# Batch 0's q and k loaded in two parts of tokens, its v loads cast on the way, and batch 1's x transposed pair by pair, in a fused attention and MLP kernel

## The chip, the cores and the metric

The kernel runs on one core of a Trainium2 chip. The metric is the device time of one execution in microseconds. Five instruction streams run beside each other and are tied by semaphores: TensorE (PE, with its weight loads shown as PEld), VectorE (DVE), ScalarE (ACT), GpSimd (POOL) and SyncE (SP). Transfers between HBM and the core's memory are issued from the streams of SP, ACT and POOL and are moved by 16 DMA engines. Each stream executes its instructions in the order in which the program lists them.

## The reference

Causal attention with 16 extra keys and values ("beacons") ahead of the sequence, then a two-layer MLP with a squared relu:

```python
B, H, S, Nb, D = (8, 8, 576, 16, 64)          # q, k, v: B x H x S x D, float32
k_all = concatenate([beacon_k, k], axis=2)
v_all = concatenate([beacon_v, v], axis=2)
scores = matmul(q, k_all.T) / sqrt(D)          # token i sees the 16 beacons and the tokens 0 to i
a = softmax(scores)
attn = matmul(a, v_all)                        # heads side by side: x is 4608 x 512
out = (relu(x @ w_in) ** 2) @ w_out            # w_in 512 x 2048, w_out 2048 x 512
```

## The kernel before, in words

The program is not written in the order in which it runs. Each piece of work is an `Op` with the engines that may do it, an assumed duration, a priority, the ops that it needs and the buffers that it takes (`Order.add`, L149). `Order.run` (L155) plays the ops through with these assumed durations and emits the instructions in the order that this gives, so a duration in the code (`act`, L384; `cost` values in the `add` calls) sets only the order of the streams. What really happens is timed by the semaphores between the instructions.

The work per batch `b` is four pairs of heads (`pr`, two heads of 64 make 128 columns).

- **q and k of batches 0 to 2** are loaded "strided" (`add_strided`, L580): partition `p` of 96 holds the six tokens 6p to 6p+5 of a head, so that a run in HBM is 1536 bytes. Batch 0's first pair comes by one load from SP and one from ACT as float32 (L592); the other pairs by one k and one q load each on POOL's queue, which cast to bf16 (L599, six loads for batch 0). PE transposes each pair (`tp`: L638 with 64 columns each for batch 0's pairs 1 to 3, L635 with 128 columns where DVE or ACT has first regrouped the two heads, the "spin" of L623), DVE copies the k half to `kT` (L650) and DVE or ACT the q half to `qT` (L655); all copies show line L437 (ACT) or L439 (DVE, POOL).
- **v** comes in five tiles of 128 keys (`add_load`, L468). Batch 0's tiles 0 to 2 are issued by SP (L483 the beacon, L484), tiles 3 and 4 and all of batch 1's by POOL (`SOFT_V`, L457). All land as float32 in one of eight staging buffers (`stg`) and are then cast into `vb` by POOL, tiles 0 and 1 of batch 0 by POOL or DVE (L508). `vb` has 65 columns per head, the last one ones, so that the product also gives the softmax sum.
- **Scores** (L764), exp on ACT (L781), causal mask on DVE (L799, L803), the product with v on PE (`av`, L819), division on DVE (L834, L835) into `xn`. Batch 0 alone is split in two phases (`SPLIT`, L686): phase 0 covers the tokens 0 to 239 and needs v tiles 0 and 1, phase 1 the rest and all five tiles.
- **x**: `xn` has to be transposed into `xT`. Batch 0 does it on PE (`add_xt_pe`, L873: transposes L883, copies L895), batches 1 to 7 by DMA transposes issued from SP, one for each of five token tiles and all four pairs (`add_xt`, L859).
- **MLP** in nine chunks of 512 tokens (`add_chunk`, L922). "s1" multiplies x by w_in (L947) in 16 blocks of 128 hidden columns, relu on ACT (L964) or DVE (L966), square on DVE (L973); "s2" multiplies by w_out (L987). Chunk 0's s1 is cut at token 240 like batch 0's phases. w_in and w_out each come in four loads on POOL's queue (L908, L917); a quarter of w_in is four blocks of s1.

Two things fix the order of POOL's stream around the start. The loads of batch 0's q and k have priorities near -200 and go first; `TURNS` (L306) chains what follows: `win0`, the v tiles 3 and 4, `win1` to `win3`, then batch 1's beacon, k, q and v, then w_out, then batch 2. And `win0` carries an explicit wait (`sync`, L911) until the last q load of batch 0 has landed, v tile 0 one until pair 1's q has landed (L1072). Where the plan finds PE idle between its microseconds 10 and 22 it puts in products of the identity that nobody reads ("fill", L526, lines L533 to L537).

## Time and profile before

| | |
|---|---|
| median of three runs | 338.75 us (338.75 to 340.36) |
| the profiled execution's own time | 338.65 us |
| its span in the trace | 336.9 us |
| busy in the span: PE, ACT, DVE, POOL | 327.1, 193.6, 160.5, 86.8 us |
| HBM read, written | 37.22 MB, 9.44 MB |
| granted TensorE clock | 1.00 throughout |

A row of a timeline or of the chain of waits is: start in us, length in us, engine, line of the code, operation, what it writes and reads, how often (xN), and in brackets how long the engine had stood idle before it and what ended that. The chain of waits follows the last instruction back, at each step to what released it. A row of the table by stretches gives for each engine the busy us and the number of instructions. "SPq" and "POOLq" are the streams that issue transfers. The time outside the span is 338.65 - 336.9 = 1.75 us.

### The profile page before, as it was taken

What the parts mean: (1) busy time and instruction counts of PE and PEld (TensorE: products, weight loads), DVE (VectorE), ACT (ScalarE), POOL (GpSimd) and SP (SyncE); (2) the same over time, 40 slices, a digit from 0 to 9 for tenths busy, and PEclk for the clock granted to TensorE, in tenths of its full rate; (3) what the DMA queues carried; (4) which work ended last, traced back from release to release, by engine and by line L of the source; (5) the groups of instructions that cost most, each with busy time, mean ns of one, the idle gap of its engine ahead of it and who ended that gap; (6) DMA issues with size and microseconds to landing.
All of it is one profiled execution on the core that took longest, in us unless ns stands there. A gap on an engine that the chain in (4) does not pass through costs nothing.

```text
span 336.9 us, 7692 instructions
## 1 busy us (share of the span) xinstructions
PE 327.1 (97%) x3172; PEld 184.2 (55%) x3172; DVE 160.5 (48%) x323; ACT 193.6 (57%) x300; POOL 86.8 (26%) x135
## 2 busy tenths in 40 slices
PE   3999999999999999999999999999999999999995
PEld 2778766545545555554468845545554544444444
DVE  6669977267604761475245632673246503301400
ACT  3887974597457647465656745755656226515611
POOL 7765911425122605140512351220000000000000
PEclk9999999999999999999999999999999999999999
DMA  9999999699959999799989996991310041011003
GB/s 167 196 207 210 206 203 207 147 247 179 221 104 223 241 199 176 185 208 228 206 121 257 242 210 138 209 196 32 104 62 2 14 120 63 0 62 64 0 17 110
DMA packets 138211, 50.38 MB, mean 150 GB/s; under 512 B 124176, under 2 KB 133264, under 8 KB 138176
## 3 DMA queue, kind: packets, MB, share of 16 engines
q1 hardware_dynamic: 128304, 40.42, 57.7%
q0 software_dynamic: 9520, 9.11, 16.3%
q8 instruction: 25, 0.41, 0.6%
q10 hardware_dynamic: 352, 0.36, 0.4%
q14 instruction: 10, 0.08, 0.1%
HBM read 37.22 MB, written 9.44 MB: 138 GB/s over the span
## 4 chain that ended last, share of the span: by engine, by line
PE 93%; DMA 2%; POOL 1%; DVE 1%; issue 1%; ACT 0%; POOLq 0%
PE ps L947 37%; PE ps L987 36%; PE ps L819 9%; PE ps L764 8%; DMA qk_area<-in_q_dram 2%; PE ps L635 1%; PE ps L1030 1%; POOL qk_area L599 1%; PE ps L883 1%; DVE g L966 0%; PE ps L537 0%; POOL vb L439 0%; PE ps L533 0%; POOL w_in L908 0%; DVE g L973 0%
## 5 line engine op out<-in xcount | busy, mean ns | idle before, releaser
L947 PE MATMUL ps<-xT,w_in 128*128 128x512 bf16 (+3 forms) x704 | 133.7, 340 | 0.2
L987 PE MATMUL ps<-w_out,g 128*128 128x512 bf16 x560 | 128.4, 379 | 0.0
L781 ACT ACTIVATE pt<-ps 128x1024 bf16<-128x1024 f32 (+3 forms) x128 | 102.9, 874 | 18.3 <-PE ps L764 18.1
L947 PEld LDWEIGHTS <-w_in 128*128 128x128 bf16 x704 | 65.9, 98 | 55.2 <-issue 3.9
L964 ACT ACTIVATE g<-ps 128x512 bf16<-128x512 f32 (+2 forms) x116 | 65.5, 568 | 39.1 <-PE ps L947 38.6
L987 PEld LDWEIGHTS <-g 128*128 128x128 bf16 x560 | 52.1, 98 | 61.1 <-issue 3.6
L973 DVE TENSOR_TENSOR g<-g 128x1024 bf16<-128x1024 bf16 (+2 forms) x80 | 52.1, 654 | 69.6 <-ACT g L964 69.4
L437 ACT COPY osb<-ps 128x512 f32<-128x512 f32 (+2 forms) x37 | 21.3, 576 | 68.8 <-PE ps L987 54.6
L439 POOL CAST qk_area<-stg 128x512 bf16<-128x512 f32 (+2 forms) x50 | 34.2, 688 | 67.5 <-DMA stg<-in_q_dram 41.0
L439 POOL CAST vb<-stg 128x512 bf16<-128x512 f32 (+1 forms) x39 | 26.1, 675 | 63.3 <-DMA stg<-in_v_dram 63.2
L799 DVE TENSOR_TENSOR pt<-pt,tri 128x1024 bf16<-128x1024 bf16 (+1 forms) x36 | 23.5, 654 | 34.2 <-ACT pt L781 34.2
L819 PEld LDWEIGHTS <-pt 128*128 128x128 bf16 (+1 forms) x960 | 34.2, 98 | 6.3 <-ACT pt L781 0.4
L966 DVE TENSOR_SCALAR g<-ps 128x512 bf16<-128x512 f32 (+2 forms) x44 | 26.8, 611 | 19.7 <-PE ps L947 19.4
L819 PE MATMUL ps<-vb,pt 128*128 128x65 bf16 (+1 forms) x960 | 35.6, 195 | 0.4 <-POOL vb L439 0.3
L764 PE MATMUL ps<-qT,kT 64*128 64x80 bf16 (+6 forms) x680 | 32.9, 235 | 0.0
L764 PEld LDWEIGHTS <-kT 64*128 64x128 bf16 x680 | 19.0, 96 | 16.8 <-issue 13.8
L835 DVE TENSOR_TENSOR xn<-ps,rcp 128x640 bf16<-128x640 f32 (+2 forms) x36 | 27.0, 750 | 1.8 <-DVE rcp L834 0.5
L834 DVE RECIPROCAL rcp<-ps 128x10 f32<-128x10 f32 (+2 forms) x36 | 7.5, 209 | 28.9 <-PE ps L819 28.9
L437 ACT COPY qT<-ps 128x576 bf16<-128x576 bf16 x12 | 7.6, 644 | 8.4 <-PE ps L635 7.4
L803 DVE TENSOR_TENSOR pt<-pt,tri 80x160 bf16<-80x160 bf16 x32 | 11.1, 347 | 0.0
L439 DVE COPY kT<-ps 128x576 bf16<-128x576 bf16 x12 | 8.9, 751 | 1.8 <-PE ps L638 1.2
L635 PE MATMUL ps<-ident,sparek 96*128 96x96 bf16 x18 | 1.5, 229 | 5.8 <-DVE sparek L439 5.8
(52 smaller groups left out, 80.4 us busy)
## 6 DMA issues: line engine op xcount, KB each, us to landing
out_dram<-osb SPq DMA_DIRECT2D x17, 512.0 KB, 3.6
stg<-in_v_dram SPq DMA_DIRECT2D x20, 256.0 KB, 5.1
stg<-in_q_dram SPq DMA_DIRECT2D x20, 256.0 KB, 5.5
stg<-in_k_dram SPq DMA_DIRECT2D x15, 256.0 KB, 4.3
w_in<-in_moe_w_in_dram POOLq DMA_DIRECT2D x4, 512.0 KB, 8.8
w_out<-in_moe_w_out_dram POOLq DMA_DIRECT2D x4, 512.0 KB, 11.6
stg<-in_v_dram SPq DMA_DIRECT2D x7, 224.0 KB, 4.5
qk_area<-in_k_dram POOLq DMA_DIRECT2D x4, 288.0 KB, 11.5
```

The source lines that it names most:

```text
L437: nc.scalar.copy(dst, src)
L439: eng[e].tensor_copy(dst, src)
L764: nc.tensor.matmul(st[:, hj, lo + col:lo + col + t1 - t0], kT[x.b % 2][hp, x.pr, 128 * c:128 * c + 128], qT[x.b % 2][hp, x.pr, t0:t1], sta ...
L781: nc.scalar.activation(pt[x.take_pt.held[0]][:, :, off:off + width], pair(box["qk"], k)[:, :, lo:lo + width], AF.Exp, bias=0.0, scale=scale)
L799: nc.vector.tensor_tensor(out=d, in0=d, in1=tri[:, m0:m0 + m, :][:, None].to_broadcast([128, 2, m, 128]), op=ALU.min)
L819: nc.tensor.matmul(a[:, hj, (t - tl[0]) * (D + 1):(t - tl[0] + 1) * (D + 1)], P[0:rr, hj, o:o + 128], vb[b % 2][0:rr, c, h, :], start=(c = ...
L835: nc.vector.tensor_tensor(out=xn[b % 2].rearrange("p t (h d) -> p h t d", d=D)[:, 2 * pr:2 * pr + 2, tl[0]:tl[0] + nt], in0=a[:, :, :, 0:D ...
L947: nc.tensor.matmul(h[:, lo - spans[0][0]:hi - spans[0][0]], w_in_sb[:, mc, ft * 128:(ft + 1) * 128], xT[:, mc, lo % RING:lo % RING + hi - lo],
L964: nc.scalar.activation(dst, h, AF.Relu, bias=0.0, scale=1.0)
L966: nc.vector.tensor_scalar(out=dst, in0=h, scalar1=0.0, scalar2=None, op0=ALU.max)
L973: nc.vector.tensor_tensor(out=d, in0=d, in1=d, op=ALU.mult)
L987: nc.tensor.matmul(o, G[:, fc, ts * 128:(ts + 1) * 128], w_out_sb[:, fc, :], start=(fc == 0), stop=(fc == NFT - 1))
```

## The change

It edits the start of the kernel and some bookkeeping:

- Batch 0 leaves `add_strided` for a new `add_first`. Its q and k come in two parts of tokens: part a, the tokens 0 to 239 on 40 partitions, part b, the tokens 240 to 575 on 56 partitions. Part a of the first pair comes from SP and ACT as before, part a of pairs 1 to 3 by one k and one q load on POOL; part b by four loads on POOL (pairs 0 and 1, pairs 2 and 3). There is one set of transposes and two copies for each pair and part. Scores of phase 0 need part a alone, those of phase 1 also part b.
- All v loads of batches 0 and 1 are issued by POOL and cast on the way into `vb` (whose rows become 66 columns per head); the staging buffers and the casting instructions fall away for them.
- `TURNS` now orders POOL's queue from the start, with v tiles 0 and 1 between the two parts and `win0` between the two halves of part b. The explicit waits of `win0` and of v tile 0 are gone.
- Unread products start at the plan's microsecond 0.6 instead of 10, before 2.6 as 512-column products of a zeroed area of `xT` ("hot", one more DVE memset).
- Batch 1's x is transposed pair by pair, three DMA transposes for each pair (12 in place of 5), each after that pair's division alone. `xn` is laid out by pairs for it.
- Batch 2's regrouping copies go from DVE to POOL. Some assumed durations of the plan are new.

```diff
-    FILL = (10.0, 22.0)
+    FILL = (0.6, 22.0)
...
-TURNS = ("win0 ld0v3 ld0v4 win1 win2 win3 bkl1 sld1k0 sld1q0 sld1k2 sld1q2 ld1v0 ld1v1 ld1v2 ld1v3 ld1v4 "
-         "wout0 wout1 wout2 wout3 bkl2 sld2k0 sld2q0 sld2k2 sld2q2")
+TURNS = ("sld0k1a sld0q1a ld0v0 ld0v1 sld0k0b sld0q0b win0 sld0k2b sld0q2b ld0v2 ld0v3 ld0v4 win1 win2 win3 bkl1 sld1k0 sld1q0 sld1k2 sld1q2 ld1v0 ld1v1 ld1v2 ld1v3 ld1v4 wout0 wout1 wout2 wout3 bkl2 sld2k0 sld2q0 sld2k2 sld2q2")
...
-    vb = [sb(f"vb{i}", [128, NT, H, D + 1], BF16) for i in range(2)]
+    vb = [sb(f"vb{i}", [128, NT, H, D + 2], BF16) for i in range(2)]
...
-        return 0.066 + n / 1200.0
+        return 0.105 + n / 1190.0
...
+    hot = xT[:, 0, 0:512]
+    nc.vector.memset(hot, 0.0)
...
+    XPAIR = 1
-    SOFT_V = [(0, 3), (0, 4)] + [(1, c) for c in range(NT)]
+    SOFT_V = [(b, c) for b in range(2) for c in range(NT)]
+    FIRST_GROUPS = [(1, 4)]
+    SECOND_GROUPS = [(0, 2), (2, 4)]
...
+            def emit_soft(e):
+                to = vb[b % 2][:, c, :, 0:D]
+                insts = []
+                if lo:
+                    insts.append(queue.dma_start(out=to[0:Nb], in_=beacon[b].transpose([1, 0, 2])))
+                insts.append(queue.dma_start(out=to[lo:rows], in_=t[b, :, t0:t0 + rows - lo, :].transpose([1, 0, 2])))
+                return insts
...
+        if now < 2.6:
+            def emit(e):
+                nc.tensor.matmul(ps[:, 7, :], hot[:, 0:128], hot, start=True, stop=True)
...
+    PARTS = [(0, 40), (240, 56)]
+    P0 = PARTS[0][1]
...
+        for n, x in enumerate("kq"):
+            def emit(e, x=x):
+                queue = nc.sync if e == "SP" else nc.scalar
+                return [queue.dma_start(out=first[x], in_=src_of[x][0, 0:2, 0:P0 * NS].rearrange(
+                    "h (p s) d -> p h s d", s=NS))]
...
+        for u, groups in ((0, FIRST_GROUPS), (1, SECOND_GROUPS)):
+            tok, parts = PARTS[u]
+            for lo, hi in groups:
+                for x in "kq":
+                    def emit(e, x=x, lo=lo, hi=hi, u=u, tok=tok, parts=parts):
+                        return [nc.gpsimd.dma_start(
+                            out=at[x][u][0:parts, 2 * lo:2 * hi],
+                            in_=src_of[x][0, 2 * lo:2 * hi, tok:tok + NS * parts].rearrange("h (p s) d -> p h s d", s=NS))]
...
+                tp = add(f"tp0.{pr}{'ab'[u]}", "PE", 0.3 if turned else 0.35, emit_tp,
+                         prio=100.0 * pr - 190 + 1000.0 * u, deps=need + [ident_op], take=("ps", "tp", [1]),
+                         mode="full" if turned else "columns")
...
+                spin[x].append(add(f"spin{b}{x}{pr}", "POOL" if b == 2 else "DVE", {"POOL": 0.85, "DVE": 0.45}, emit_spin,
...
+            if b == 0:
+                late_deps[p] = [trans[0, "k"][HP + pr], trans[0, "q"][HP + pr]]
...
+    def add_xt_pairs(b):
+        at = (b * S) % RING
+        for pr in range(HP):
+            for n, (lo, hi) in enumerate(((0, 1), (1, 4), (4, 5))):
...
+                    nc.sync.dma_start(out=dst, in_=area[0:rows, 128 * (NT * pr + lo):128 * (NT * pr + hi)], transpose=True)
...
+                        deps=[norm_ops[HP * b + pr, 0]] + ring_deps(b * S + t0, b * S + t0 + cols), dma=0.16 * cols / 128,
...
-            w_ops["in", i] = add(f"win{i}", "POOL", 0.95, emit, prio=-100 + i, sync=[strided[0][HP - 1, 'q']] if i == 0 else (),
+            w_ops["in", i] = add(f"win{i}", "POOL", 0.95, emit, prio=-100 + i, 
...
-                if c == 0:
-                    sync = [strided[0][HP - 3, "q"]]
+                pass
...
-            add_xt(b)
+            (add_xt_pairs if b == XPAIR else add_xt)(b)
...
-    named["ld1v0"].behind.append(named["cast0v4"])
```

More of the change, by code (lines that the diff above doesn't have):

```diff
@@ L537, in emit @@
                     nc.tensor.matmul(ps[:, spot, 0:128], ident, ident, start=True, stop=True)
-        op = Op("fill", "PE", 0.11, emit, mode=mode)
+        op = Op("fill", "PE", 0.22 if now < 6.0 else 0.11, emit, mode=mode)
         op.left, op.held = 0, None
@@ L589, in add_strided @@
[L589 to L595 removed]
+        step = 2
+        for pr in range(0, HP, step):
@@ L713 @@
     norm_ops = {}
+    late_deps = {}
     def add_pair(b, pr):
```

150 lines of the change are left out of this document (106 added, 44 removed).

## The prediction

> **What bounds the kernel now.** First the table by stretches and one row of PE's timeline:
>
> ```profile
> 0.00:19.59 19.59, 13.28 (x188) 10.14 (x188) 12.75 (x45) 12.36 (x18) 13.60 (x27) 1.00 0.99 185
> 19.59:46.25 26.66, 26.49 (x406) 20.87 (x403) 23.76 (x61) 22.50 (x43) 17.75 (x25) 1.00 1.22 207
> 46.25:66.00 19.75, 19.75 (x248) 11.79 (x246) 11.44 (x27) 9.41 (x15) 5.44 (x10) 1.00 1.00 180
> ```
>
> ```profile
> 19.59 0.99 PE L947 MATMUL ps<-xT,w_in 128*128 128x240 bf16 x8
> ```
>
> I cut the stretches at 19.59 us, where the first product of the MLP runs, and at 46.25 us, where s2 of chunk 0 begins. From 19.59 us on PE is busy without a gap (26.49 of 26.66 us, then 19.75 of 19.75). Before it PE runs 188 instructions in 19.59 us, against 406 in the next 26.66. So time can be won almost only ahead of 19.59 us, and what is won there stays won as long as PE never lacks work later. The chain of waits over the first 20 us says what sets 19.59 (its first line gives shares of these 20 us):
>
> ```profile
> by line: DMA qk_area<-in_q_dram 28.3%; POOL qk_area L599 14.8%; issue 11.2%; PE ps L764 6.5%; PE ps L819 5.8%; PE ps L883 5.5%; PE ps L537 5.3%; POOL vb L439 4.4%; PE ps L533 3.9%; POOL w_in L908 3.9%; DVE xn L835 2.2%; PE ps L947 2.1%; POO
> ...
> 4.99 5.65 DMA qk_area<-in_q_dram
> 10.64 0.29 issue
> 10.93 0.77 POOL w_in L908
> ...
> 12.60 0.88 POOL vb L439
> 13.48 0.04 issue
> 13.52 0.50 PE ps L819 x6
> ```
>
> POOL's stream stood at `win0` until the last q had landed, so its cast of a v tile came at 12.60, and PE's first product with v at 13.52. From there to the MLP are 6.07 us (19.59 - 13.52), of which about 1.85 us are unread products (L537 and L533, 5.3% and 3.9% of 20 us).
>
> **Part 1: q and k in two parts.** Timelines of DVE, of ACT (one row) and, from 2 to 4 us, what the DMA engines moved:
>
> ```profile
> 1.57 0.27 DVE L410 MEMSET bks<- 128x256 uint32 x1
> 1.92 0.59 DVE L411 MEMSET tri<- 128x640 bf16 x1
> 2.48 1.65 DVE L416 MEMSET pt<- 128x96 uint32 x12
> 5.19 0.56 DVE L439 CAST sparek<-g 96x768 bf16<-96x768 f32 x1 [1.05 <-DMA g<-in_k_dram]
> ```
>
> ```profile
> 8.88 0.79 ACT L781 ACTIVATE pt<-ps 128x736 bf16<-128x736 f32 x1
> ```
>
> ```profile
> DMA packets 383, 0.52 MB, mean 259 GB/s; under 512 B 48, under 2 KB 383, under 8 KB 383
> ```
>
> The first pair's two loads are 2 x 2 x 576 x 64 x 4 bytes = 0.59 MB, 2.3 us at 259 GB/s; part a is 240/576 of it, 0.25 MB or 0.95 us. So it lands 1.3 us earlier, 3.9 instead of 5.19. But DVE's memsets end at 2.48 + 1.65 = 4.13, and the change adds one of the size of the 0.27 us row: DVE is free at 4.4. The regrouping copies (0.56) then end at 5.0, 0.8 us sooner than now. Two copies of 240 columns in place of 576 save about as much again, so the first exp comes near 7 instead of 8.88. Part a of pairs 1 to 3 is 6 heads x 240 x 64 x 2 bytes each of k and q, 0.37 MB in bf16, which the 0.82 MB in 4 us of a row below moves in 1.8 us: from 4 to 6, seen near 7, all three together, where the last q now lands at 10.64. All this lies ahead of the v tiles below and is hidden by them: it sets nothing unless v comes more than 2 us earlier than I reckon.
>
> [...] No row of before shows a 40-partition load.
>
> The part b transposes are added PE work: 24 more instructions for each pair.
>
> ```profile
> 32.22 0.51 PE ps L635 x12
> ```
>
> That is a pair of batch 1: twelve transposes of 96 columns, all 128 wide. Batch 0's pairs 1 to 3 have 24 of half the width; split in 40 and 56 columns a pair costs 0.51 again if columns count, 1.02 if instructions do. Of four pairs two fall behind the start of the MLP; I charge **0.6 us** (0 to 1.0).
>
> **Part 2: POOL's queue.** It now reads: k and q of part a; identity (0.30); mask matrix `tri` (priority -150, so ahead of v, 1.48); v tile 0 with its beacon; v 1; part b of pairs 0 and 1; `win0`; part b of pairs 2 and 3; v 2 to 4; `win1` to `win3`. POOL's timeline has the prices:
>
> ```profile
> 2.85 0.30 POOL masks.py:199 TENSOR_SCALAR_AFFINE_SELECT ident<-ident 128x128 bf16<-128x128 bf16 x1
> ...
> 5.88 1.48 POOL L424 TENSOR_SCALAR_AFFINE_SELECT tri<-tri 128x128 bf16<-128x128 bf16 x5
> 10.93 0.77 POOL L908 DMA_DIRECT2D w_in<-in_moe_w_in_dram  x1 [3.56 <-DMA qk_area<-in_q_dram]
> 11.70 0.91 POOL L484 DMA_DIRECT2D stg<-in_v_dram  x1
> ```
>
> The first two issues end ahead of the identity, as now. `tri` therefore ends at 2.85 + 0.30 + 1.48 = 4.63, the beacon at 5.2, v 0 is issued 5.2 to 6.1 and v 1 to 7.0 (0.91 each). How long until bytes flow? `win0` was issued at 10.93:
>
> ```profile
> q1 hardware_dynamic: 1318, 0.33, 83.7%
> q0 software_dynamic: 5, 0.00, 1.1%
> ```
>
> ```profile
> q1 hardware_dynamic: 709, 0.18, 41.1%
> q0 software_dynamic: 96, 0.10, 39.9%
> ```
>
> These are the queues at 10 to 12 and at 12 to 14 us (packets, MB, share of the 16 engines); q1 is SP's, q0 POOL's. POOL's queue moves five packets in the first and a 40% share in the second, so it begins near 13.0, 2.1 us after the issue. v 0 thus flows from 7.3. **A casting v load** is not in the trace. Bounds: below, bytes of the bf16 side at the rate of the other casting loads; above, SP's v loads, 0.33 MB in 2 us, which is 1.55 us for 256 KB. POOL's queue from 32 to 36 us, mostly uncast v loads, and from 20 to 24 us, casting loads of weights and k:
>
> ```profile
> q0 software_dynamic: 294, 0.84, 104.0%
> ```
>
> ```profile
> q0 software_dynamic: 830, 0.82, 124.0%
> ```
>
> 0.84 MB in 4 us is 1.25 us for 256 KB; 0.82 MB is 0.63 us for 128 KB. I take 1.25: the source still comes in runs of 256 bytes. v 1 then ends near 9.9 and is seen 0.8 us later (the first pair's k was moved by 4.4 and landed at 5.19), at **10.8**. No cast follows, so PE's product with v starts at 10.8 instead of 13.52: 2.7 us earlier (9.5 to 12.0 by the bounds and one us on the start).
>
> [...]
>
> **Part 3: from v to the MLP.** The 6.07 us shrink by what of the 1.85 us of unread products isn't needed, and grow where DVE now makes part b's copies in the same stretch. I take 5.3 (4.2 with all the fill gone, 7.0 with four copies of some 0.4 us on the path): the MLP starts at 16.1 instead of 19.59, a **lead of 3.5 us** (0.6 to 4.7; `win0`, issued 8.2, is served behind v 0, v 1 and part b until 14.1 and lands near 14.9).
>
> **Part 4: does PE stay fed?** Until 22 us only a quarter of w_in is there. On POOL's timeline:
>
> ```profile
> 24.94 0.85 POOL L484 DMA_DIRECT2D stg<-in_v_dram  x1 [1.91 <-DMA w_in<-in_moe_w_in_dram]
> 27.44 2.73 POOL L484 DMA_DIRECT2D stg<-in_v_dram  x3 [1.65 <-DMA w_in<-in_moe_w_in_dram]
> ...
> 31.96 0.80 POOL L917 DMA_DIRECT2D w_out<-in_moe_w_out_dram  x1 [0.36 <-DMA qk_area<-in_k_dram]
> 33.59 1.55 POOL L917 DMA_DIRECT2D w_out<-in_moe_w_out_dram  x2 [0.82 <-DMA qk_area<-in_q_dram]
> ```
>
> ```profile
> DMA to landing us min/median/max: 9.8/11.6/13.8
> ```
>
> POOL stands at 24.94 and 27.44 for w_in, at 31.96 and 33.59 for batch 1's k and q, each the eighth load back. The queue is at its rate (207 GB/s from 19.59 on), so what counts is bytes ahead. They are the same in both orders; the slack at 10 to 14 us (0.33 and 0.28 MB in 2 us each, against 0.41) goes, and a like one opens between part a, served by 6, and v 0 at 7.3. So `win2` and `win3` (24.9, 27.4), batch 1's k and q (32.0, 33.5) and the first of w_out stay within 0.5 us of now. In the lead, from 16.1 to 22, PE has two pairs' part b (1.0), eight or nine pieces of phase 1's scores (the chain's four at L764 take 6.5% of 20 us, so 2.6 to 2.9), four blocks of s1 (16 products, 1.8 by the row of 19.59), and products with v once tiles 2 to 4 are in near 19.7: about 6 us of work for 6. I charge **0.2 us** (0 to 2). Later, s2 starts at 46.25 - 2.7 = 43.5 and needs w_out's first quarter, which lands at 41.8 now (issued 31.96, and the second fence gives the four w_out loads' time to landing; the first has the least, 9.8). Batch 1's x:
>
> ```profile
> xT<-xn SPq DMA_TRANSPOSE x35, 2.5
> ```
>
> ```profile
> 58.99 6.50 SPq L866 DMA_TRANSPOSE xT<-xn  x5
> ```
>
> ```profile
> 67.05 1.03 PE L947 MATMUL ps<-xT,w_in 128*128 128x512 bf16 x4
> ```
>
> The fourth of five, the last that chunk 1 needs, is issued from 62.9 (58.99 + 3 x 1.3) and lands 2.5 us later at 65.4, 1.6 us ahead of chunk 1's first product at 67.05. Moved forward by 2.7 us, PE would wait for it by 1.1 us if batch 1 did not move too; of twelve smaller ones only three stand behind the last division, some 3.9 us of SP's stream if each costs the 1.3 of now, instead of 5.2 for four. That edit is therefore worth 0 to 1.1 us, and I count it as cover. SP has nothing else queued there but batch 3's loads.
>
> Batch 2's regrouping on POOL (eight copies) is covered: POOL is busy 5.44 of 19.75 us there and loses five casts. The new durations of the plan change orders only; 0.5 us either way. The unread products run while PE has nothing else; one of 512 columns, under 0.5 us, could stand ahead of a real one, covered by the v tiles. If they bring a faster clock to the first transposes, that too lies ahead of v; the granted clock is 1.00 in every row of the table, so nothing shown here prices it. The 66-column rows are never read at their end: 0.
>
> **The sum.** 338.65 - 3.5 + 0.6 + 0.2 = **335.95**, say 335.9; the profiled execution is 0.10 us below the median of 338.75. With the bounds of the terms its own range is 334.6 to 337.4.
>
> **Rivals.**
>
> 1. *Casting halves the v loads.* At 0.63 us each v 1 is seen 1.2 us earlier and `win0` too; the lead grows to its limit of 4.7, less 0.6 of transposes: 338.65 - 4.1 = 334.5. For it: all other casting loads run at their bf16 bytes. Against: those come in runs of 1536 bytes.
> 2. *The lead is eaten before `win1`.* Phase 1 has twelve exps of some 0.85 us (8.88: 0.79 for the smaller ones), 10 us of ACT from near 12.6; if PE's stream stands behind them and v tiles 2 to 4 for 2 us more than charged, 338.65 - 2.7 + 2 = 338.0. For it: ACT's load; against: ACT is busy 12.36 of the first 19.59 us, so it has room.
> 3. *One queue, slower v loads: slower than before.* If a casting load costs twice 1.25 us (each run written in two steps), ten of them stand ahead of w_out, whose first quarter lands at 41.8 + 12.5 = 54.3, and PE, out of work near 46.25, waits until then: +8, up to 346. It decides where ten loads eat the slack of 46.25 - 41.8 = 4.4 us, from 1.7 us a load. Against: the dearest row is 1.55.
> 4. *The order doesn't come out as written*, because the plan's streams misjudge the chip and PE sits behind a late instruction: the gain of rival 2, counted there.
>
> **How the numbers follow.** Forecast 0.5, rival 1 0.2, rivals 2 and 4 0.17, rival 3 0.13. A measurement can tell 0.5% (1.7 us) from no change: faster means under 337.0. Faster: nearly all of the forecast's half and rival 1, 0.7; same: the upper end of the forecast and rival 2, 0.17; slower: rival 3, 0.13. The range takes in rivals 1 and 2 with their bounds and the near edge of 3: 333.2 to 338.7.
>
> **What would show it.** Right: first product with v (L819) near 10.8 with no cast ahead, first L947 near 16, s2 (L987) near 43.5, and from there the same lead to the end; POOL's queue near 200 GB/s from 7 us on. Part 1 is wrong if the first exp comes after 8; part 2 if a v load takes much over or under 1.25 us or `tri` is not ahead of v 0; part 3 if L947 starts after 17.5; part 4 if PE shows gaps between 16 and 27 us or ahead of chunk 1. The forecast falls if the lead at the first L947 is not the lead at the end, or if w_out lands after s2 could start.

## The result, and the profile after

The changed kernel is slower: 343.39 us (341.11 to 344.67) beside 339.22 us (338.75 to 340.36) for the kernel before, a ratio of 1.0121 (95% interval 1.0091 to 1.0152). The prediction was 335.9 us in a range of 333.2 to 338.7. The profiled execution took 342.73 us with a span of 341.0 us, 4.1 us more than before's 336.9, and the reading below follows these 4.1 us.

The changed kernel by stretches, cut where the first product of the MLP runs, where s2 of chunk 0 begins and where chunk 1 begins:

```profile
0.00:18.87 18.87, 16.38 (x263) 12.07 (x264) 11.39 (x44) 8.83 (x17) 14.89 (x28) 0.82 1.16 131
18.87:48.30 29.43, 29.43 (x494) 23.48 (x492) 25.38 (x69) 25.38 (x45) 13.51 (x19) 1.00 1.45 197
48.30:69.07 20.77, 20.55 (x249) 12.01 (x250) 9.79 (x19) 10.07 (x16) 11.25 (x17) 1.00 0.89 147
```

The MLP starts at 18.87 instead of 19.59: a lead of 0.7 us, not 3.5. From there to s2 it takes 29.43 us instead of 26.66, and s2 starts 2.05 us late (48.30 against 46.25). PE is "busy" in all 29.43 us, with 494 instructions where before had 406. This is the first thing to see: the busy share does not show the loss, because other work fills it. The 88 more are 48 transposes of part b, 20 unread products and 20 products of scores; the last are scores of phase 1, which before ran ahead of the MLP. PE's work on scores in this stretch, of the changed kernel (104 by its weight loads) and of before (84):

```profile
18.87:48.30 29.43, 6.38 (x104) 2.93 (x104) 1.00 1.45 197
19.59:46.25 26.66, 4.78 (x88) 2.30 (x84) 1.00 1.22 207
```

The chain of waits over the same 29.43 us stays on PE alone, so here nothing but PE's own stream of work sets when s2 starts:

```profile
by line: PE ps L1070 50.8%; PE ps L861 18.6%; PE ps L916 13.0%; PE ps L734 7.0%; PE ps L565 5.4%; PE ps L665 3.0%; PE ps L1006 2.0%; PE ps L597 0.3%
```

Chunk 1 starts 2.02 us late (69.07 against 67.05), and chunk 2 4.06 us late. These are the rows of chunk 2 on PE's timeline, of before and of the changed kernel:

```profile
105.04 2.33 PE L947 MATMUL ps<-xT,w_in 128*128 128x512 bf16 x10
```

```profile
109.10 3.18 PE L1070 MATMUL ps<-xT,w_in 128*128 128x512 bf16 x13 [1.54 <-DMA xT<-xn]
```

Behind chunk 2 the two kernels run alike: 341.0 - 109.10 = 231.9 us against 336.9 - 105.04 = 231.9. So there are two losses, about 2.0 us up to s2 and another 2.0 us between chunk 1 and chunk 2.

The chain of waits of the changed kernel over its first 20 us:

```profile
by line: DMA qk_area<-in_q_dram 28.1%; PE ps L565 22.2%; PE ps L665 13.7%; PE ps L861 12.1%; issue 5.7%; PE ps L916 5.1%; PE ps L1006 4.0%; PE ps L1070 3.6%; POOL qk_area L631 2.5%; POOLq L1251 0.1%
...
7.91 0.36 PE ps L665 x12
8.28 0.34 PE ps L861 x4
...
10.44 0.97 PE ps L565 x8
11.41 0.72 PE ps L861 x6
12.13 1.18 PE ps L565 x10
13.32 0.66 PE ps L916 x12
13.98 1.74 PE ps L565 x20
```

L565 is the unread product, L665 a transpose of q and k, L861 the scores, L916 the product with v. POOL's wait for q and the cast of v are gone from the chain, as predicted. In their place stands PE's own stream: 22.2% of 20 us, 4.4 us, are unread products, which PE executes in the order of the plan whether or not v has landed. Ahead of all this stands the first pair's regrouping, which ends at 5.79:

```profile
4.96 0.83 ACT L438 CAST sparek<-g 40x768 bf16<-40x768 f32 x1 [2.01 <-DMA g<-in_k_dram]
```

**The first loss** is seen best on ACT. First before, then the changed kernel (L781 and L878 are the exps; four in phase 0 of batch 0, with 736 columns, then twelve in phase 1, with 832 or 928; a row's shape is that of its first instruction):

```profile
12.45 3.23 ACT L781 ACTIVATE pt<-ps 128x736 bf16<-128x736 f32 x4
16.76 0.36 ACT L437 COPY xT<-ps 128x240 bf16<-128x240 bf16 x1 [1.09 <-PE ps L883]
17.56 3.30 ACT L781 ACTIVATE pt<-ps 128x832 bf16<-128x832 f32 x4 [0.44 <-PE ps L764]
...
25.93 1.94 ACT L781 ACTIVATE pt<-ps 128x928 bf16<-128x928 f32 x2
```

```profile
11.87 1.46 ACT L878 ACTIVATE pt<-ps 128x736 bf16<-128x736 f32 x2 [0.60 <-PE ps L861]
15.86 0.36 ACT L438 COPY xT<-ps 128x240 bf16<-128x240 bf16 x1 [2.53 <-PE ps L1006]
...
18.01 3.43 ACT L878 ACTIVATE pt<-ps 128x832 bf16<-128x832 f32 x4
...
21.94 2.61 ACT L878 ACTIVATE pt<-ps 128x928 bf16<-128x928 f32 x3
24.94 1.70 ACT L878 ACTIVATE pt<-ps 128x928 bf16<-128x928 f32 x2 [0.39 <-PE ps L861]
27.27 1.70 ACT L878 ACTIVATE pt<-ps 128x832 bf16<-128x832 f32 x2 [0.63 <-PE ps L861]
29.57 0.86 ACT L878 ACTIVATE pt<-ps 128x832 bf16<-128x832 f32 x1 [0.59 <-DVE rcp L931]
```

Before, the row at 12.45 holds three exps of phase 1: their scores ran while PE waited for v, and the first of the three starts at 13.3. In the changed kernel the first exp of phase 1 comes at 18.01. ACT does no exp between 13.3 and 18.0, stands still for 2.53 us of it, and then needs until 29.57 + 0.86 = 30.4 for the same twelve; before they ended at 25.93 + 1.94 = 27.9. That is 2.6 us later, at the place where PE needs them for its products with v.

Two things hold these scores back. One is POOL's queue, where part b stands behind v. The last load that pairs 0 and 1 need (q, issued at 7.78) lands 5.2 us after its issue, at 13.0, where before the last q of all was in at 10.64:

```profile
L631 POOL DMA_DIRECT2D qk_area<-in_q_dram x1: 659/659/659, 7.8 to 7.8; - x1
DMA to landing us min/median/max: 5.2/5.2/5.2
```

The other is PE's own order: the transposes of this part b come only at 15.93, some 3 us after it has landed, behind the product with v and the unread products of the chain above. From the transposes to the exp are 2.1 us (18.01 - 15.93). Had they followed the landing at once, the exp would have come near 15.1, an estimate from these rows; of the 4.7 us by which it is later than before, 1.8 would then be the queue's and 2.9 those of PE's order. (In the kernel a2 below, which has no unread products, these transposes come at 14.2 and the exp at 17.3, and the granted clock rises only at 25.6.) Pairs 2 and 3 are alike: landed at 17.9 (issued at 9.85, 8.1 us), transposed from 20.46.

PE's rows there, of the changed kernel:

```profile
15.93 0.56 PE L665 MATMUL ps<-ident,qk_area 56*64 56x56 bf16 x24
...
16.82 0.56 PE L665 MATMUL ps<-ident,qk_area 56*64 56x56 bf16 x24
...
20.46 0.94 PE L665 MATMUL ps<-ident,qk_area 56*64 56x56 bf16 x48
...
22.86 0.50 PE L565 MATMUL ps<-ident 128*128 128x128 bf16 x6
...
25.33 0.73 PE L565 MATMUL ps<-ident 128*128 128x128 bf16 x10
```

Part b's transposes, 2.06 us in all, now lie on PE's path to s2, where before all of q and k was transposed by 11.8 us, ahead of v. And between 22.9 and 25.9 PE fills in unread products. The second quarter of w_in was no help: POOL, which stands until it has landed, went on at 23.69 instead of 22.5 or earlier, and at 26.24 and 28.83 (before 24.94 and 27.44) for the third and fourth:

```profile
23.69 0.54 POOL L490 DMA_DIRECT2D vb<-in_beacon_v_dram  x1 [0.84 <-DMA w_in<-in_moe_w_in_dram]
```

**The second loss** shows on SP. Its stream in the changed kernel (L988: batch 1's x by pairs, L963: batch 2's by tiles), then before (L866: both by tiles):

```profile
46.52 8.59 SPq L988 DMA_TRANSPOSE xT<-xn  x6
...
57.72 3.99 SPq L988 DMA_TRANSPOSE xT<-xn  x3
...
65.06 4.60 SPq L988 DMA_TRANSPOSE xT<-xn  x3
...
94.71 5.67 SPq L505 DMA_DIRECT2D stg<-in_q_dram  x4
...
101.32 7.71 SPq L963 DMA_TRANSPOSE xT<-xn  x5
```

```profile
92.34 7.84 SPq L866 DMA_TRANSPOSE xT<-xn  x5
```

Twelve transposes by pairs take 8.59 + 3.99 + 4.60 = 17.2 us of SP's stream; five by tiles took 6.50 us. One transpose took much the same time whether by pair (one or three blocks of 128 columns; least, median and most in ns below) or by token tile (1250 to 1283 ns), but for two of 2.07 us:

```profile
L988 SPq DMA_TRANSPOSE xT<-xn x12: 1093/1236/2072, 46.5 to 68.4; - x12
```

Batch 2's x starts at 101.32 instead of 92.34, 9.0 us later, and chunk 2 waits 1.54 us for it. SP is one reason for these 9.0 us, and not the larger. Batch 2's last division, before and in the changed kernel:

```profile
90.03 0.82 DVE L835 TENSOR_TENSOR xn<-ps,rcp 128x640 bf16<-128x640 f32 x1
95.96 0.82 DVE L932 TENSOR_TENSOR xn<-ps,rcp 128x640 bf16<-128x640 f32 x1
```

It comes 5.9 us later, so batch 2's attention is itself late. Behind it SP takes 4.5 us until it turns to this x (101.32 - 96.78), before 1.5: the other 3.0 us are SP's written order, which now has later loads (94.71 to 101.2) ahead of it. Why batch 2's attention falls back more than s2 did was not tested.

### The profile page after: what moved, and what is told of

It is laid out like the page before. It is cut to its first block, busy times and chain, and to the rows that moved or that the text cites. A ratio compares the mean times of both kernels' runs of the same rounds, so it can differ in the third digit from the quotient of the medians.

```text
span 341.0 us, 7981 instructions
## 1 busy us (share of the span) xinstructions
PE 331.1 (97%) x3294; PEld 188.3 (55%) x3335; DVE 160.8 (47%) x326; ACT 193.0 (57%) x297; POOL 89.6 (26%) x138
## 4 chain that ended last, share of the span: by engine, by line
PE 91%; DMA 4%; SPq 1%; issue 1%; DVE 1%; ACT 1%; POOL 0%; ACTq 0%; POOLq 0%
PE ps L1070 37%; PE ps L1110 33%; PE ps L916 8%; PE ps L861 8%; DMA xT<-xn 2%; PE ps L565 2%; DMA qk_area<-in_q_dram 2%; SPq L963 1%; PE ps L734 1%; PE ps L665 1%; PE ps L1153 1%; ACT pt L878 1%; PE ps L1006 0%; DVE pt L896 0%; SPq L988 0%
## 5 line engine op out<-in xcount | busy, mean ns | idle before, releaser
L1110 PE MATMUL ps<-w_out,g 128*128 128x512 bf16 x539 | 125.0, 379 | 1.3 <-issue 0.2
L878 ACT ACTIVATE pt<-ps 128x1024 bf16<-128x1024 f32 (+3 forms) x128 | 103.0, 871 | 38.3 <-PE ps L861 37.5
L1070 PEld LDWEIGHTS <-w_in 128*128 128x128 bf16 x704 | 65.1, 98 | 56.0 <-issue 6.4
L1087 ACT ACTIVATE g<-ps 128x512 bf16<-128x512 f32 (+2 forms) x111 | 62.9, 567 | 47.9 <-PE ps L1070 47.5
L440 POOL CAST qk_area<-stg 128x512 bf16<-128x512 f32 (+2 forms) x50 | 31.9, 643 | 63.8 <-DMA stg<-in_q_dram 36.6
L1089 DVE TENSOR_SCALAR g<-ps 128x512 bf16<-128x512 f32 (+2 forms) x49 | 29.8, 607 | 22.7 <-PE ps L1070 22.3
L916 PEld LDWEIGHTS <-pt 128*128 128x128 bf16 (+1 forms) x960 | 33.7, 98 | 5.5
L916 PE MATMUL ps<-vb,pt 128*128 128x65 bf16 (+1 forms) x960 | 35.0, 194 | 0.1
L440 POOL CAST vb<-stg 128x512 bf16<-128x512 f32 (+1 forms) x30 | 21.1, 707 | 50.1 <-DMA stg<-in_v_dram 37.1
L861 PE MATMUL ps<-qT,kT 64*128 64x80 bf16 (+6 forms) x680 | 32.4, 232 | 0.0
L861 PEld LDWEIGHTS <-kT 64*128 64x128 bf16 x680 | 18.4, 95 | 17.1 <-issue 14.6
L438 ACT COPY qT<-ps 128x576 bf16<-128x576 bf16 (+2 forms) x13 | 6.7, 531 | 8.2 <-PE ps L734 4.7
L440 DVE COPY kT<-ps 128x576 bf16<-128x576 bf16 (+2 forms) x16 | 9.4, 603 | 3.7 <-PE ps L665 2.2
L491 POOL DMA_DIRECT2D vb<-in_v_dram x10 | 8.8, 886 | 4.1 <-DMA w_in<-in_moe_w_in_dram 3.8
L900 DVE TENSOR_TENSOR pt<-pt,tri 80x160 bf16<-80x160 bf16 x32 | 9.4, 295 | 0.0
```

The lines of the kernel that those rows point to most:

```text
L438: nc.scalar.copy(dst, src)
L440: eng[e].tensor_copy(dst, src)
L861: nc.tensor.matmul(st[:, hj, lo + col:lo + col + t1 - t0], kT[x.b % 2][hp, x.pr, 128 * c:128 * c + 128], qT[x.b % 2][hp, x.pr, t0:t1], sta ...
L878: nc.scalar.activation(pt[x.take_pt.held[0]][:, :, off:off + width], pair(box["qk"], k)[:, :, lo:lo + width], AF.Exp, bias=0.0, scale=scale)
L916: nc.tensor.matmul(a[:, hj, (t - tl[0]) * (D + 1):(t - tl[0] + 1) * (D + 1)], P[0:rr, hj, o:o + 128], vb[b % 2][0:rr, c, h, 0:D + 1], star ...
L1070: nc.tensor.matmul(h[:, lo - spans[0][0]:hi - spans[0][0]], w_in_sb[:, mc, ft * 128:(ft + 1) * 128], xT[:, mc, lo % RING:lo % RING + hi - lo],
```

## The experiments

Each ratio is to the kernel before on the same chip, with its 95% interval.

**First set: one part of the changed kernel undone at a time, and one part alone.**

*a1_x_by_tiles*: batch 1's x by tiles again.
```diff
-    XPAIR = 1
+    XPAIR = 99
```


> The changed kernel with batch 1's x transposed by five token tiles again, all else as changed. Theory 'SP's stream': the twelve transposes by pairs hold SP for 17 us in place of 6.5 (about 1.33 us each, whether of one tile or of three), batch 2's v and batch 3's and 4's loads queue behind them, and the lag grows from 2.0 us at chunk 1's first product to 4.1 at chunk 2's. Then this kernel gains 1.5 to 2.5 us on the changed one, chunk 2's first product comes near 107, and the lag at chunk 2 is what it is at the start of s2 (2 us). Rival 'the start decides': all of the loss is work missing by 48 us and the transposes only show it; then the time stays within 0.5 us of the changed kernel's, and some other wait takes the place of the one on xT. Rival 'pairs are cover': without them chunk 1 waits for x, 1 us slower.


Measured 344.18 us, 1.0152 (1.0128 to 1.0176): no gain. Chunk 2 no longer waits for x, but the order of the streams changes with the edit, and chunk 1 now starts late instead (72.6).

*a2_no_fill*: no unread products at all.
```diff
-    FILL = (0.6, 22.0)
+    FILL = (0.0, 0.0)
```


> The changed kernel without any unread product (neither the early ones nor those up to 22 us). Theory 'fill on a cold clock': between 10 and 15.7 us the unread products stand in PE's in-order stream at half clock (4.2 us of the chain of waits), so without them the first product with v comes near 11.5 instead of 13.1 and the MLP's first product near 17 instead of 18.9; the end comes 1 to 2 us sooner. Rival 'PE has nothing else': the products only fill time in which data is missing; the first product of the MLP moves by less than 0.5 us. Rival 'they keep the clock': the clock rises later than at 15.5 us (18 in the kernel before), real products run longer cold, and the end comes 0 to 2 us later.


Measured 344.89 us, 1.0172 (1.0144 to 1.0199). The first product with v comes at 11.9 and the MLP at 18.0, the earliest so far: 1.2 us of the delay at v were the unread products. But the granted clock rises only at 25.6, and s2 starts at 51.3. What the products cost ahead of v they may give back as clock; this run changes both at once.

*a3_spin_dve*: batch 2's regrouping on DVE again.
```diff
-                spin[x].append(add(f"spin{b}{x}{pr}", "POOL" if b == 2 else "DVE", {"POOL": 0.85, "DVE": 0.45}, emit_spin,
+                spin[x].append(add(f"spin{b}{x}{pr}", "DVE", {"POOL": 0.85, "DVE": 0.45}, emit_spin,
```


> The changed kernel with batch 2's regrouping copies on DVE again. Theory 'POOL is off the path': batch 2's transposes, which end at 64.9 against 61.2 before, end 2 to 4 us sooner, but its scores wait for the end of chunk 0's s2 anyway: time the same within 0.5 us. Rival 'late copies are the second loss': batch 2's products with v and its x come 2 us sooner, and the time falls by 1.5 to 2 us.


Measured 344.14 us, 1.0163 (1.0135 to 1.0191): this edit is covered, as predicted.

*b1_x_by_pairs*: the kernel before with batch 1's x by pairs and nothing else.
```diff
+    XPAIR = 1
...
-            add_xt(b)
+            (add_xt_pairs if b == XPAIR else add_xt)(b)
```


> The kernel before with only one part of the change, batch 1's x by pairs (twelve transposes). Theory 'SP's stream': SP is held some 10 us longer between 45 and 66 us, loads behind it come later, and the kernel is 1 to 2 us slower than before. Rival 'pairs are cover or harmless': within 0.7 us of before.


Measured 339.98 us, 1.0049 (1.0022 to 1.0075): slower by some 1.7 us. In its trace chunk 1 starts 1.5 us sooner than before (65.58), of which s2 already had 0.6 (45.6; the granted clock rose at 13.7 in this execution, at 17.8 in before's); chunk 2 starts 1.4 us later (106.46), and SP turns to batch 2's x at 99.01 instead of 92.34, though batch 2's last division ends only 1.6 us later (92.48). Here SP's order is the larger part: pairs win where they are and lose more behind.

**Second set: is it the clock, the plan's durations, or the queue?** a0 repeats the changed kernel for comparison.

*a0_again*:


> The changed kernel unaltered, on the chip and beside the runs of before that the other three share. All theories: 343 to 345 us. It says how far its own runs lie apart, and whether the granted clock rises at the same place in every execution (4.9 us, back at 8.3, again at 15.2 in the first profile; 16.1 in two kernels with the same start).


Measured 343.84 us, 1.0162 (1.0125 to 1.0198). Its profiled execution was its slowest (347.4 us), so its rows below lie later than a usual run's.

*a4_old_durations*: the plan's old durations.
```diff
-        return 0.105 + n / 1190.0
+        return 0.066 + n / 1200.0
```
(and the like for `eq`, `norm` and the copies of x)


> The changed kernel with the old assumed durations of the plan (exp and relu on ACT, the division, the copies), nothing else. Batch 1's last product with v comes 12.7 us after the start of s2 in every kernel of the changed family and 9 to 9.7 us after it in the kernels that keep the old durations. Theory 'the new durations push batch 1 back': with the old ones it comes 9 to 10.5 us after, and 1 to 2 us of the 2.1 us lost between s2's start and chunk 2 come back. Rival 'the start does it': batch 1's place follows from the order of loads, the distance stays above 12 us and the time within 0.7 us of the changed kernel's.


Measured 343.01 us, 1.0125 (1.0098 to 1.0151): up to 0.4% better than a0, with overlapping intervals.

*a5_more_products*: six products of 80 columns ahead of each transposes set of batch 0, and twice the fill until 14 us.
```diff
-            for i in range(2):
+            for i in (0, 1, 0, 1) if now < 14.0 else (0, 1):
...
+                    for _ in range(6):
+                        nc.tensor.matmul(bank(box["t"])[:, 170:250], ident, ident[:, 0:80], start=True, stop=True)
```


> The changed kernel with more unread products up to 14 us: six of 80 columns ahead of each of batch 0's eight sets of transposes, and four in place of two where the plan is idle. Theory 'cold clock': the fall back to half clock at 8.3 us and the rise only at 15 to 16 us is what makes PE's in-order stream late, so a clock held from 5 us on brings the MLP's first product from 18.8 to 17 or sooner, s2's start from 48.2 to 46.5 to 47 and the end 1 to 2 us sooner. Rival 'the products themselves are in the way': the clock rises earlier, but the first product of the MLP comes no sooner or later. If the clock does not rise earlier the run tells nothing of either.


Measured 341.16 us, 1.0069 (1.0044 to 1.0094). The clock rises at 5.7 and stays; yet s2 starts at 50.7. Its order of the later streams has no wait for x, unlike a0. A clock that is up from 5.7 on does not bring the lead back.

*a6_win1_first*: the second quarter of w_in ahead of v tiles 2 to 4.
```diff
-... sld0q2b ld0v2 ld0v3 ld0v4 win1 win2 ...
+... sld0q2b win1 ld0v2 ld0v3 ld0v4 win2 ...
```


> The changed kernel with the second quarter of w_in ahead of batch 0's v tiles 2 to 4 on POOL's queue. Theory 'the lead is eaten by missing data': PE has only four blocks of s1 until the second quarter lands (near 23.5), so with it near 19.5 four more blocks run before 23 us, fewer unread products stand between 22 and 26 us, and s2 starts 0.5 to 1.5 us sooner. Rival 'v tiles are the tighter ones': phase 1's products with v come 2.5 us later, batch 0's x with them, and s2 starts no sooner or up to 1 us later.


Measured 344.52 us, 1.0147 (1.0119 to 1.0176); s2 at 51.5. The second quarter landed at 20.8 instead of 23.4, but v tiles 2 to 4 landed 2.5 to 2.8 us later, so the run says that this exchange loses, not that PE had enough of w_in between 22 and 26.

**Third set: do the prices add up?** Tiles with old durations, the same with a5's products, and the early unread products alone on the kernel before.

*a7_tiles_old_durations* (a1's and a4's edits), *a8_tiles_old_more* (a7's and a5's):


> The changed kernel with two parts undone together: batch 1's x by token tiles, and the old assumed durations. Each alone left the time where it was (344.2 and 343.0). Theory 'one late x, passed on': the new durations put batch 1's last product with v 12.7 us behind s2's start in place of 9 to 10, so its x is late for chunk 1 by 2 us; the transposes by pairs repair that and hold SP so long that batch 2's x is late for chunk 2 by the same 2 us. Undoing one moves the wait, undoing both removes it: 1.5 to 2.5 us sooner than the changed kernel (341 to 342), no wait of 1 us or more on xT ahead of chunk 1 or 2. Rival 'the start of the kernel makes x late': a wait of about 2 us remains ahead of chunk 1 or chunk 2, time 343 to 344.

> As the kernel before it in this list, and with the additional unread products of the experiment that held the clock from 5.7 us on and gained 2.7 us (341.2). Theory 'one late x' and 'cold clock' add up: 339 to 340, level with the kernel before. Rival 'that gain was the same wait': the additional products gained because their plan happened to have no late x, so here nothing is added: within 0.7 us of a7.


Measured 342.01 us, 1.0084 (1.0053 to 1.0115) and 341.29 us, 1.0086 (1.0055 to 1.0117). Half of the loss goes, and it is the second half: in a7 s2 is still 2.6 us late (48.9), but chunk 2 no later than that (2.6 us, 107.6), where the changed kernel had gone from 2.0 to 4.1 and a0 from 3.7 to 7.1. By this, a5's gain was the same late x; its products add nothing to a7.

*b2_early_products*: the kernel before with the early unread products. *b3_more_products*: also more of them, as in a5.
```diff
-    FILL = (10.0, 22.0)
+    FILL = (0.6, 22.0)
...
+    hot = xT[:, 0, 0:512]
+    nc.vector.memset(hot, 0.0)
...
```


> The kernel before with only the early unread products of the change (and their memset). Theory 'cold clock': the clock rises at 5 us and again, for good, near 15 instead of 18; the MLP's first product comes 0.5 to 1 us sooner, as in the run of x by pairs, whose clock rose at 13.7 by chance (18.6 instead of 19.6), and the time falls 0.3 to 1 us. Rival 'they are in the way': no sooner, or up to 1 us later.

> The kernel before with the early unread products and, up to 14 us, more of them: six of 80 columns ahead of each of batch 0's four sets of transposes, four in place of two where the plan is idle. Theory 'cold clock': the clock holds from 5 to 6 us on, PE's lead at 28 us is 1 us or more and stays; 337.5 to 338.5. Rival 'they are in the way': the clock holds, but the first product with v, which waits for v at 13.3, comes no sooner, and the time is that of before or worse.


Measured 341.25 us, 1.0070 (1.0046 to 1.0094) and 341.03 us, 1.0075 (1.0044 to 1.0107). b2 by stretches, cut where its granted clock changes:

```profile
7.28:10.70 3.42, 3.23 (x96) 2.57 (x94) 2.58 (x5) 3.11 (x6) 0.88 (x3) 1.00 1.27 231
10.70:14.11 3.41, 1.66 (x23) 0.76 (x20) 2.27 (x5) 3.22 (x6) 3.41 (x5) 1.00 1.06 172
14.11:17.52 3.41, 3.04 (x34) 1.92 (x34) 3.25 (x13) 2.43 (x4) 2.39 (x4) 0.50 1.15 237
17.52:20.94 3.42, 3.42 (x28) 2.00 (x26) 1.28 (x5) 2.67 (x3) 2.98 (x5) 0.50 1.23 209
```

With the early products the clock rises at 7.28, where PE waits for data anyway. From 10.70 to 14.11 PE is busy for 1.66 of 3.41 us, at 14.11 the clock falls, and the half rate (0.50) now lies on the stretch from v to the MLP and lasts to 20.94, where the kernel before was back at full rate at 17.82.

**Fourth set: what remains when pairs, new durations and early products are all gone?** By the theory of the third set, next to nothing.

*c1_parts_and_casts* (a7 with `FILL = (10.0, 22.0)`), *c2_late_products* (the changed kernel with that alone), *c3_products_from_6* (c1 with `FILL = (6.0, 22.0)`):


> The changed kernel with unread products from the plan's microsecond 10 on, as before, batch 1's x by tiles and the old durations: what is left of the change is q and k in two parts, the cast v loads, POOL's order and batch 2's regrouping. No unread product stands ahead of the first product with v. Theory that the prices add up: a7_tiles_old_durations had 1.0084 and the early products alone on the kernel before cost 0.0070, so 1.000 to 1.003 here, the first product with v near 11 and s2 near 46 to 47. Theory of the prediction, that the lead was only blocked by the early products: 0.990 to 0.994, the MLP starting near 16 and s2 near 43.5. Theory that the two parts and the casts cost by themselves: still 1.006 or more.

> The changed kernel with its one constant for the unread products put back (from the plan's microsecond 10), pairs and new durations kept. If the prices add up: a0_again's 1.016 less 0.007, so 1.007 to 1.011, with the lateness of batch 2's x (1 us or more between 100 and 112) still there. If the early products matter only together with the pairs: near 1.016 or near 1.003.

> c1_parts_and_casts with the unread products from the plan's microsecond 6 on: some 38 products more, ahead of the first product with v and between the scores. If products on a cold clock ahead of v are what costs: the first product with v 1 us or more later than in c1, the time 0.002 to 0.006 above c1. If what costs is the clock's rise and fall through the products of the very first microseconds: as c1 or up to 0.003 below it, since the clock then rises once, near 14, and stays.


Measured 342.12 us, 1.0093 (1.0069 to 1.0116); 344.14 us, 1.0155 (1.0130 to 1.0179); 341.58 us, 1.0082 (1.0060 to 1.0104). The theory that the prices add up fell, and so did the prediction's own: with no unread product ahead of it the product with v starts at 11.82 in c1, 1.7 us sooner than before, and the kernel is as slow as a7. Early products cost 0.7% in the kernel before and nothing here. c1's PE:

```profile
11.82 0.49 PE L916 MATMUL ps<-vb,pt 128*128 128x65 bf16 x6 [0.19 <-ACT pt L878]
...
14.57 0.84 PE L665 MATMUL ps<-ident,qk_area 56*64 56x56 bf16 x24
...
15.98 0.85 PE L665 MATMUL ps<-ident,qk_area 56*64 56x56 bf16 x24
...
18.85 1.01 PE L1070 MATMUL ps<-xT,w_in 128*128 128x240 bf16 x4
```

From the first product with v to the MLP are 7.0 us, not 5.3 as predicted nor 6.07 as before: two sets of part b's transposes ahead of the clock's rise at 20.65 (0.84 and 0.85; the two behind it take 0.56 each), scores of phase 1, and ten unread products (1.07 us of the chain). And it is no longer v that this first product waits for: v 1 has landed at 10.7, and the row names the exp (ACT pt).

*c4_none_after_17* (c3 with `FILL = (6.0, 17.0)`), *c5_after_none_after_17* (the changed kernel with `FILL = (0.6, 17.0)`), *c6_none_after_12* (c3 with `FILL = (6.0, 12.0)`): the unread products at 22 to 26 us go, in c6 also those ahead of the MLP.


> c3_products_from_6 with no unread product after the plan's microsecond 17: the 18 that stand behind the start of the MLP, about 1.5 us of PE between 22 and 26 us, go. If they stand ahead of work whose data are there, the lag of 1.3 us that arises at 22 to 26 us goes and the ratio is 0.003 to 0.005 below c3's 1.0082, so 1.003 to 1.005. If PE waits there for data in any case, gaps take their place on PE's timeline and the ratio stays within 0.002 of c3's.

> The changed kernel with no unread product after the plan's microsecond 17, all else as it is. If those 18 cost what they last: 1.011 to 1.013 in place of 1.012 to 1.016, and s2 about 47 in place of 48.3. If PE waits there for data: as before, with gaps in place of the products.

> c4_none_after_17 without the ten unread products that stand ahead of the first product of the MLP as well (0.7 us of PE at 17.5 in c3). If they are on the path: the MLP starts 0.4 to 0.7 us sooner than in c4 and the ratio is 0.001 to 0.002 lower. If PE only waits there for x: no difference, unless the granted clock falls.


Measured 340.92 us, 1.0066 (1.0045 to 1.0086); 345.15 us, 1.0160 (1.0122 to 1.0199); 341.04 us, 1.0061 (1.0039 to 1.0083). Taking them out brings 0.002 at most: gaps stand where they stood. In c6, where they are all gone between 18 and 26, one row of PE, and from the chain of waits between the first product of the MLP (18.03) and s2 (47.30) the shares and the first of the exps:

```profile
23.43 0.38 PE L861 MATMUL ps<-qT,kT 64*128 64x208 bf16 x4 [0.48 <-DVE g L1089]
```

```profile
by line: PE ps L1070 34.8%; PE ps L916 10.9%; ACT pt L878 8.8%; PE ps L861 8.6%; DVE g L1089 5.5%; DVE kT L440 5.4%; PE ps L734 5.2%; DVE g L1096 5.0%; issue 3.0%; DVE xn L932 2.8%; PE ps L1006 2.8%; DVE pt L896 2.0%; ACT g L1087 1.4%; DVE 
...
17.98 2.59 ACT pt L878 x4
```

The chain now leaves PE: 8.8% of 29.27 us are exps, nearly all in the first four of phase 1. In the changed kernel it never left PE there. c6 has the lowest ratio of all versions with the two parts, not told apart from c4's and a5's, and it is still slower than before; no version here beats the kernel before.

**One number runs through all of them**: the end of batch 0's last exp, read on ACT's timeline, beside the start of s2 (its first weight load), in us, for eleven of the kernels and one execution of each.

| | 5th exp starts | last exp ends | s2 starts |
|---|---|---|---|
| b1 (q and k whole) | 13.3 | 26.9 | 45.6 |
| before (whole) | 13.3 | 27.9 | 46.2 |
| b2 (whole) | 13.0 | 28.7 | 47.6 |
| c3 | 17.6 | 29.7 | 47.1 |
| c6 | 17.9 | 29.9 | 47.0 |
| changed kernel | 18.0 | 30.4 | 48.2 |
| a7 | 18.5 | 31.0 | 48.9 |
| c1 | 17.8 | 31.3 | 48.6 |
| a0 | 19.7 | 32.1 | 49.9 |
| c2 | 17.6 | 32.8 | 51.2 |
| a2 | 17.3 | 32.8 | 51.3 |

The fifth exp is the first that needs part b. Every kernel with q and k whole starts it by 14.5, every kernel in two parts at 17.3 or later, whatever its clock, its unread products or its x. Over all traces but b3's, which has a clock fall of its own at 41 us, s2 starts 17.0 to 19.6 us after the last exp; so the later exp goes with the later s2, though not in every pair (b2 against c3 and c6). This is a relation over traces, and which of the two drives the other it does not say: exps wait for scores, and scores for their place in PE's stream. Two experiments would show what holds phase 1 back, and neither was run: part b ahead of the v tiles in the same queue, and part b's transposes as soon as it has landed in PE's order.

## Why the prediction was wrong, point by point

1. **Part 1, first half.** DVE was free at 4.4 as predicted, but part a was not there: k was seen at 4.96 and q at 5.24 instead of 3.9, only 0.2 to 0.3 us sooner than before, with 42% of the bytes. The regrouping ended at 5.8, not 5.0. And the first exp came at 9.09, not near 7: the plan had put pair 1's transposes ahead of pair 0's scores (7.91 and 8.28 in the chain), and they waited for pair 1's q. That this start is "hidden" by the v tiles and "sets nothing unless v comes more than 2 us earlier than I reckon" failed as well: in c1 v was in at 10.7, about as reckoned, and the first product with it waited for the exps until 11.82.
2. **Part 1, part b: the step that failed.** I charged 0.6 us for the transposes as such. They cost PE 2.06 us (four sets of about 0.5; 2.8 in c1, where two sets lie ahead of the clock's rise) on its path, since before they lay in PE's wait for v. Above all I did not ask what is late next. Phase 1's twelve exps, which I took to run "from near 12.6" in rival 2, need part b and start at 18.0; their scores, 20 products of which ran ahead of the MLP before, lie behind its start. "ACT is busy 12.36 of the first 19.59 us, so it has room" was the error in one line: that room was before 18 us, and the change took the work out of it. Two parts were meant to let phase 0 begin sooner, but its first exp came no sooner than before (9.09 against 8.88), and phase 1 paid. That phase 1's work moved behind the start of the MLP is read from the rows; how much of it is the queue and how much PE's order stays open.
3. **Part 2**: the landing was right, the product was not. The first casting v load was issued at 5.04 (predicted 5.2), and v 1 landed at 10.5 by the trace's landing records (predicted to be seen at 10.8). But the first product with v came at 13.1, since 0.97 + 1.18 us of unread products, at a granted clock of 0.50 (8.33 to 15.15), and scores, stand ahead of it in PE's stream; in c1, without them, it came at 11.82. The price of 1.25 us for a casting load has no one value in the trace: v 1 landed 1.8 us behind v 0, batch 1's tiles 0 to 3, at 36 to 38 us, 0.82 us apart on average. No run shows the two steps of writing that rival 3 supposes. Neither rival 1 nor rival 3 came of it, because v no longer set the end.
4. **Part 3**: from the first product with v to the MLP 5.8 us, close to the predicted 5.3. The lead of 3.5 us became 0.7, since the product came 2.3 us later than reckoned; with it in time, in c1, the stretch grew to 7.0 and the lead was 0.7 again. The most that any version in two parts had was 1.6 (a2, 17.99; c6, 18.03). 0.7 lies within my bounds for the lead (0.6 to 4.7); the range of the sum, up to 337.4, left that lower bound out.
5. **Part 4**: "PE stays fed". From the MLP's start to s2 are 29.43 us instead of 26.66, 2.8 us more where 0.6 + 0.2 were charged. That is near the 2 us of rival 2, "the lead is eaten before win1", but not by its mechanism: PE's stream does not stand there, it carries the transposes, scores and unread products of the 88 more instructions. My sign for part 4, gaps on PE, could not show this. And what I gave as a rival to the lead came on top of a lead that was not there. The later quarters of w_in came 1.3 us later than before, not within 0.5. x by pairs was counted "as cover", 0 to 1.1 us: it won some 0.9 us at chunk 1 in b1 and lost that and more at chunk 2, since I looked at the transposes' own time and not at what SP's written order has behind them.
6. **Unread products at nothing.** On the kernel before they cost 0.7% (b2). In the changed kernel their removal changes nothing (a2, c2, c5): waits take their place, in c6 for exps and for DVE, and in a2 the clock stays low longer.
7. **The new durations** at 0.5 us either way: the runs put them, with the pairs, at 0.6% (c2 against c1) to 0.8% (a0 against a7) together; what each costs alone in the changed kernel is not settled (undoing the pairs alone, a1, brought 0.1%, the durations alone, a4, 0.4%).

In the span, -3.5 + 0.6 + 0.2 = -2.7 us was forecast and +4.1 measured. Of the 6.8 us between, 2.8 are the lead (points 1 to 4), 2.0 the way from the MLP's start to s2 (points 2 and 5) and 2.0 lie between chunk 1 and chunk 2, where PE waits for x (point 5).

So the 1.2% to 1.6% is, by the runs, about 0.9% for q and k in two parts with the cast v loads in one queue and batch 2's regrouping on POOL (c1), and about 0.6% for x by pairs with the new orders (c2 against c1). What the casts cost or bring without the two parts was not tried.

## What to carry to other kernels

When an input is split so that its first part comes sooner, follow the second part to the engine that needs it most: idle time ahead of the bottleneck is only room while there is work to put into it. Where a plan fixes each engine's order, filler work put where the plan sees an engine idle runs at the chip's time, not the plan's, and hides the wait from the busy share; count instructions, not busy time. A change that is good at its own place (x by pairs) has to be followed through the queue that it lengthens to the next user.

## What the runs showed of the hardware

**The granted clock changed at distances of 3.42 us, or of twice that.** In the changed kernel it goes up at 4.91, down at 8.33, up at 15.15 (distances 3.42 and 6.82); in b2 up at 7.28, down at 14.11, up at 20.94 (twice 6.83); in a0 it falls at 112.74, at the end of a stretch with a wait of 2.50 us for x, and rises at 116.16:

```profile
109.50:112.74 3.24, 0.68 (x7) 0.33 (x5) 0.00 (x0) 1.78 (x2) 0.48 (x1) 1.00 0.56 107
112.74:116.16 3.42, 3.42 (x9) 1.22 (x9) 1.88 (x4) 1.07 (x2) 0.00 (x0) 0.50 0.78 234
```

From the start of the span the changes lie differently in these executions: the first rise is at 13.7 in b1 and at 17.8 in before, which have the same start of the kernel and reach the MLP at 18.62 and 19.59. What makes the clock fall these runs do not settle. It fell behind 3.42 us in which PE was busy for 2.19 us (4.91 to 8.33 in the changed kernel) and behind 3.41 us with 1.66 us (b2), but stayed at 1.00 behind 3.42 us with 1.83 us (107.42 to 110.84 in the changed kernel, with chunk 2's wait for x).

**A clock column of 1.00 ahead of the first record is no measurement.** In c1 the first record is a rise at 20.65, and the column shows 1.00 before it. But ten unread products take 1.07 us of the chain at 17.99, and eight take 0.55 at 24.42: 107 against 69 ns. The prediction took before's 1.00 at its word, and so did the "1.00 throughout" of the table of before: its first record is a rise at 17.82, and ahead of it ten unread products of the same shape (15.13 and 16.10 in its chain) take 107 ns each as well.
